# Rows ahead of transposes, values' eviction ahead of the exponential, and a first routing one round sooner, in a kernel for attention and a mixture of experts

## Chip, cores and metric

One core of a Trainium2 chip runs the whole program. The metric is device microseconds of one execution. The core has five engines that each work through their own instructions in order: TensorE (PE) for matmuls, VectorE (DVE), ScalarE (ACT), GpSimd (POOL) and SyncE (SP), which here issues most transfers. All data is float32 at the program's edges.

## What is computed

The reference takes q, k and v of shape (8, 8, 576, 64), does attention inside chunks of 64 positions, and sends the result through a mixture of experts with one expert for each token:

```python
scores = scale * np.matmul(q_c, k_c.transpose(0, 1, 2, 4, 3))      # chunks of 64
scores = scores - np.max(scores, axis=-1, keepdims=True)
attn = np.exp(scores)
attn = attn / (np.sum(attn, axis=-1, keepdims=True) + 1e-09)
out = np.matmul(attn, v_c)
x = out.transpose(0, 2, 1, 3).reshape(B * S, H * D)               # 4608 tokens x 512
logits = x @ w_gate + modality_bias[modality_id]                  # 8 experts
e_idx = np.argmax(logits, axis=1)
gate_w = softmax(logits)[np.arange(N), e_idx]
for e in range(E):
    mask = e_idx == e
    out[mask] = gate_w[mask, None] * (np.maximum(x[mask] @ w1[e], 0.0) @ w2[e])
```

The experts' two weight matrices are 512 x 1024 and 1024 x 512.

## The kernel before

**Stages.** Attention goes over 36 tiles of 128 tokens (two chunks of 64 for each of 8 heads), two tiles a round after the first two single ones. Behind it the tokens are worked expert by expert in slots of up to 384 tokens: a slot gathers its tokens' rows, turns them, and runs 8 steps f of a first matmul (`first`, tile `hp`) and a second one (`second`, tile `yb`). Weights and rows are split into a high and a low part so that three fast matmuls stand for one exact one.

**Order.** The program switches the planner off (`manual_schedule`): every engine gets its instructions in the order in which the Python code emits them. A wait of one instruction thus holds up all that was emitted behind it on the same engine. Buffers of one tag go round in turn; a new tile waits until the readers of the buffer's last tile are done. PSUM has two buffers of tag "s" (scores `sp`; later `hp`), two of tag "t" (transposed probabilities `ap`, values `xp`, some others), and the pair `yb`.

**A tile's way** (t is the tile):
- `scores(t)`: 16 matmuls of 64 x 64 into `sp`; DVE takes the maximum `mx` and subtracts it (`ex`).
- `exps(t)`: ACT takes the exponential in place; POOL adds the two halves into a ring tile `sr`.
- `sums(t)`: DVE sums `sr` (`sm`) and takes the reciprocal (`ris`).
- `transposes(t)`: 4 PE transposes of `ex` into `ap` (tag "t"); ACT copies them to `at`. The load of a later v tile is held back by a dependency on these transposes (`load_v(..., hold)`).
- `values(t)`: 16 matmuls of v and `at` into `xp` (tag "t"); ACT copies them to `xt` (the "eviction of values").
- `rows(t)`: 8 PE matmuls that turn `xt` back to token rows and give the router's partial logits, into `yb`; DVE scales them into `xr`.
- `put(t)`: ACT copies the partial logits (`lp`) and issues the write of `xr` to the DRAM table `xd`.

**A round** for tiles a and a+1 emits: transposes(a), rows(a-2), sums(a), put(a-2), rows(a-1), sums(a+1), put(a-1), v load of a+2, transposes(a+1), v load of a+3; scores of a+2 and a+3 with the q/k loads four tiles ahead; exps(a+2); values(a), values(a+1), exps(a+3). From round 8 to 22 each round also issues two writes that clear the token table (`clear_part`).

**Jobs.** Routing is written as generators. `advance()` takes one step of every generator in `jobs` and `pooljobs`; it is called after each `values`. `advance([pooljobs])` steps only the second list, twice more a round. `route(0)` covers tiles 0 to 13 and starts in round 14: step 1 scales the partial logits (POOL), step 2 adds them up (POOL, `lg`), step 3 takes the maximum (`gmx`) and the exponential (`ge`, ACT), steps 4 and 5 count tokens of each expert along the tiles (`scan`), step 6 does nothing, step 7 multiplies for the counts across partitions (`rp`, tag "t") and computes each token's place `pi`. It ends by adding `early_table` (which experts fill the first three slots, table `e_tab`, seven steps) and `scatter` (14 indirect writes `tab` by POOL, one a step). `route(1)`, for the other 22 tiles, runs in the expert stage.

**PLAN** says what is done ahead for the first slots at which tile, as t - 36 after values(t) and `advance()`: `locate` reads a slot's list of tokens from the table (SP: a register load and a DMA `tl`; it waits for the scatters), `gather` gets their rows (POOL: copy `tk`, then one indirect DMA a tile into `xg`), `fetch` loads weights (SP), `hi` and `lo` split them (ACT, DVE). `split(k)` transposes a quarter of the gathered rows of slot 0 on PE (`tp`, three transposes, one for each gather) and splits it on ACT and DVE.

Behind the last round stand split(0), rows(34), split(1), put(34), split(2), split(3), and then slot 0, which begins with `first` and takes rows(35) after it.

Of the kernel before, what the change touches and what calls it, by code (L numbers as in the profile page):

```python
# [8 lines left out]
F32 = mybir.dt.float32  # L9
# [10 lines left out]
P = 128  # L20
N = B * S
DM = H * D
E = 8
# [11 lines left out]
BUSY = 4  # L35
PLAN = {
    -9: {"fetch": [(0, 1), (1, 1)]},
    -7: {"locate": [(0,), (1,), (2,)]},
# [29 lines left out]
NEG = 1  # L68
# [21 lines left out]
def attention_moe(ctx: ExitStack, tc: tile.TileContext, qkv, mod, cst, bias, wcat, wfst, out):  # L90
# [168 lines left out]
    def sums(t):  # L259
        sm = wk.tile([P, H], F32, name="sm")  # L260
        V.reduce_sum(sm, sring[t % 4], axis=AX.X)  # L261
        V.reciprocal(ris[:, t], sm)

    def transposes(t):
        ex = st[t]["ex"].rearrange("p h k -> p (h k)")
        ap = ps.tile([P, NP, P], F32, tag="t", name="ap")
        for p in range(NP):
            hold = PE.transpose(ap[:, p, :], ex[:, p * P:p * P + P], ident)  # L268
        at = mp.tile([P, DM], F32, tag="yo", name="at", bufs=4).rearrange("p (a c) -> p a c", a=NP)
        A.copy(at, ap)  # L270
        st[t]["at"] = at
        return hold
# [15 lines left out]
    def rows(t):  # L288
        xt, ri = st[t]["xt"], ris[:, t]

        xr = wk.tile([P, NJB, NK, 32], F32, name="xr", bufs=4)
        fp = yb[t % 2].rearrange("p b (a c) -> p (b a) c", a=2)
        for p in range(NP):
            PE.matmul(fp[:, p, 0:GWC], xt[:, p, :], gw[:, p, :], start=True, stop=True)  # L294
        rb = ri.rearrange("p (a b) -> p a b", a=NP).unsqueeze(3)
        V.tensor_tensor(  # L296
            xr.rearrange("p (b j) a d -> p a b j d", b=2),
            fp[:, :, 0:P].rearrange("p a (b j d) -> p a b j d", b=2, j=2),
            rb.unsqueeze(4).to_broadcast([P, NP, 2, 2, 32]), ALU.mult)
        st[t] = fp, xr  # L300
# [11 lines left out]
    def route(g):  # L312
        t0, n = GROUPS[g]
# [44 lines left out]
        V.tensor_scalar_add(gs, gs, 1e-9)  # L358
        tg = tgs[g]
        V.reciprocal(tg.bitcast(F32)[:, :, 1], gs)  # L360
        for _ in range(2 if g < NEG else 5):
            yield
        rp = ps.tile([P, 2, 32, E], F32, tag="t", name="rp")
        PE.matmul(rp[:, 0, 0:n], ub, oh, start=True, stop=True)
        PE.matmul(rp[:, 1, 0:n + 1], ones, scan[i][:, off:off + n + 1], start=True, stop=True)
        V.tensor_tensor(base[g + 1], base[g], rp[:, 1, n], ALU.add)
# [380 lines left out]
    busy(BUSY)  # L747

    for a, n in [(0, 1), (1, 1)] + [(t, 2) for t in range(2, NT, 2)]:
        hold = transposes(a)  # L750
        if a > 1:
            for t in (a - 2, a - 1):
                rows(t)
                sums(t + 2)
                put(t)
            load_v(a + 2, hold)
            if 8 <= a < 24:
                clear_part()
            load_v(a + 3, transposes(a + 1))
            if 8 <= a < 24:  # L760
                clear_part()
            for g, (t0, m) in enumerate(GROUPS):
                if t0 + m == a:
                    jobs.append(route(g))
        else:
            if not a:
                exps(1)
            sums(a)
        advance([pooljobs])
        small = [t for t in (range(a + 2, a + 4) if a > 1 else (a + 2,)) if t < NT]  # L770
        for t in small:
            scores(t)
            load_qk(t + NB)
        if n == 2 and small:
            exps(a + 2)
        advance([pooljobs])
        for t in range(a, a + n):
            values(t)
            if small and (n == 1 or t > a):
                exps(small[-1])  # L780
            advance()
            plan(t - NT)
        if a == 2:
            prepare()
    split(0, "s")
    rows(NT - 2)
    split(1, "s")
    put(NT - 2)
    split(2)
    split(3)  # L790
# [81 lines left out]
```

## Time and profile before

| what | value |
|---|---|
| median of three runs | 563.65 us (563.55 to 563.82) |
| the profiled execution, its own time | 564.0 us |
| its span, first to last instruction | 562.1 us |
| mean granted clock of TensorE | 0.995 |
| busy PE / DVE / ACT / POOL | 549.6 / 360.9 / 244.4 / 175.2 us |
| DMA, mean over the span | 237 GB/s |

Times in a row of the profile are microseconds from the span's start. In a timeline a row reads: start, length, engine, line, operation, tile written and tiles read, shapes, count, and in brackets how long the engine had idled and what ended that. "PEld" is TensorE's weight load, which overlaps its matmuls; "SPq" and "ACTq" are transfers issued by SP and ACT. In a list of waits a row reads: who waited, for whom, microseconds in total, how often, the longest. In a table of stretches a row reads: from and to, length, busy time and instructions of PE, PEld, DVE, ACT and POOL, the clock granted to TensorE (1.00 is full speed), the DMA engines' busy share, GB/s. The attention stage is roughly the first 138 us, the experts the rest.

### The profile page before, as it was taken

How to read it: one execution, taken by the hardware profiler on the slowest of the kernel's cores; microseconds unless marked ns; L12 is line 12 of the kernel's file. 1: busy time of each engine (PE TensorE's matmuls, PEld its weight loads, DVE VectorE, ACT ScalarE, POOL GpSimd, SP SyncE). 2: the span in 40 equal slices, each digit the busy share in tenths (PEclk: the TensorE clock that was granted, in tenths of full speed). 3: DMA queues.
4: the chain of work that ended last, by engine and by line, in shares of the span. 5: the costliest groups of instructions: out<-in, count | busy, mean ns of one | idle time of the engine just before them, and what ended most of it. 6: DMA issues, size and time to landing. Idle time of an engine off the chain costs nothing.

```text
span 562.1 us, 12401 instructions
## 1 busy us (share of the span) xinstructions
PE 549.6 (98%) x4900; PEld 499.1 (89%) x4900; DVE 360.9 (64%) x633; ACT 244.4 (43%) x422; POOL 175.2 (31%) x182
## 2 busy tenths in 40 slices
PE   8999999998999999999999999999999999999995
PEld 6999989997889899899898999899899898998994
DVE  4777798966899665655656565565655656556751
ACT  3555554556434433443534434433434434435541
POOL 3322516742658754032220412213032220402011
PEclk9999999998999999999999999999999999999999
DMA  8999999998788649776683976748586683756500
GB/s 328 326 307 315 382 339 322 300 307 320 235 265 252 224 135 309 271 238 220 158 300 132 278 245 185 266 125 281 191 257 196 187 268 121 247 187 208 188 37 26
DMA packets 61409, 133.22 MB, mean 237 GB/s; under 512 B 11230, under 2 KB 31390, under 8 KB 54944
## 3 DMA queue, kind: packets, MB, share of 16 engines
q1 hardware_dynamic: 48368, 103.08, 56.3%
q0 software_dynamic: 7072, 19.18, 10.4%
q10 hardware_dynamic: 5904, 10.11, 4.9%
q8 instruction: 40, 0.66, 0.5%
q14 instruction: 25, 0.20, 0.1%
HBM read 102.16 MB, written 30.70 MB: 236 GB/s over the span
## 4 chain that ended last, share of the span: by engine, by line
PE 75%; issue 12%; DVE 4%; POOL 3%; DMA 2%; ACT 2%; ACTq 0%; POOLq 0%; DVEq 0%
PE yb L654 29%; PE hp L641 28%; PE yb L294 6%; PE sp L247 5%; PE xp L282 4%; PE ap L268 3%; POOL out L666 1%; DMA out<-yo,tk 1%; DMA qk<-in_qkv 1%; DVE xr L296 1%; PE yb L166 1%; DVE ex L251 1%; DVE mx L249 1%; DMA v<-in_qkv 1%; ACT ex L256 1%
## 5 line engine op out<-in xcount | busy, mean ns | idle before, releaser
L616 DVE TENSOR_TENSOR wl<-raw,wh 128x1024 fp32r<-128x1024 f32 (+1 forms) x106 | 129.6, 1224 | 37.2 <-ACT wh L612 37.2
L644 ACT ACTIVATE hh<-hp 128x384 fp32r<-128x384 f32 (+1 forms) x104 | 49.4, 475 | 217.7 <-PE hp L641 215.0
L641 PE MATMUL hp<-xl,wh 128*128 128x384 f32 (+1 forms) x416 | 136.7, 328 | 0.0
L641 PE MATMUL hp<-xh,wh 128*128 128x384 f32 (+1 forms) x416 | 136.4, 328 | 0.0
L641 PE MATMUL hp<-xh,wl 128*128 128x384 f32 (+1 forms) x416 | 136.3, 328 | 0.0
L645 DVE SCALAR_TENSOR_TENSOR hl<-hp,hh 128x384 fp32r<-128x384 f32 (+1 forms) x104 | 55.7, 536 | 111.0 <-ACT hh L644 111.0
L654 PE MATMUL yb<-wh,hl 128*128 128x512 f32 x296 | 117.4, 397 | 0.5 <-DVE hl L645 0.5
L654 PE MATMUL yb<-wh,hh 128*128 128x512 f32 x296 | 117.6, 397 | 0.0
L654 PE MATMUL yb<-wl,hh 128*128 128x512 f32 x296 | 116.8, 395 | 0.0
L666 POOL DMA_INDIRECT out<-yo,tk x37 | 46.9, 1267 | 222.5 <-DVE yo L665 214.8
L612 ACT CAST wh<-raw 128x1024 fp32r<-128x1024 f32 (+1 forms) x106 | 108.6, 1026 | 0.2 <-issue 0.2
L641 PEld LDWEIGHTS hp<-xl,wh 128*128 128x128 f32 x416 | 78.3, 188 | 4.2 <-DVE xl L586 0.3
L641 PEld LDWEIGHTS hp<-xh,wh 128*128 128x128 f32 x416 | 78.3, 188 | 3.8
L641 PEld LDWEIGHTS hp<-xh,wl 128*128 128x128 f32 x416 | 78.4, 189 | 0.0
L654 PEld LDWEIGHTS yb<-wh,hl 128*128 128x128 f32 x296 | 55.9, 189 | 14.9 <-DVE hl L645 1.5
L654 PEld LDWEIGHTS yb<-wl,hh 128*128 128x128 f32 x296 | 55.7, 188 | 9.5
L654 PEld LDWEIGHTS yb<-wh,hh 128*128 128x128 f32 x296 | 55.7, 188 | 9.1 <-ACT hh L644 0.2
L544 POOL DMA_INDIRECT xg<-xd,tk x37 | 41.2, 1113 | 24.5 <-issue 15.0
L257 POOL TENSOR_TENSOR sr<-ex 128x256 f32<-128x256 f32 x36 | 26.2, 728 | 70.3 <-ACT ex L256 70.2
L385 POOL DMA_INDIRECT tab<-tg,pi x36 | 39.6, 1099 | 15.0 <-issue 9.4
L294 PE MATMUL yb<-cs,xt 128*128 128x144 f32 x288 | 40.1, 294 | 0.0
L247 PEld LDWEIGHTS sp<-qk 64*64 64x64 f32 x1152 | 35.9, 137 | 3.9 <-DVE sm L261 1.8
(126 smaller groups left out, 524.7 us busy)
## 6 DMA issues: line engine op xcount, KB each, us to landing
raw<-in_wcat SPq DMA_DIRECT2D x48, 1024.0 KB, 6.6
qk<-in_qkv SPq DMA_DIRECT2D x36, 512.0 KB, 6.6
v<-in_qkv SPq DMA_DIRECT2D x36, 256.0 KB, 4.2
xd<-xr ACTq DMA_DIRECT2D x36, 256.0 KB, 2.9
xs<-xg SPq DMA_DIRECT2D x10, 768.0 KB, 5.0
xq<-xs SPq DMA_DIRECT2D x40, 192.0 KB, 4.1
raw<-in_wfst SPq DMA_DIRECT2D x4, 512.0 KB
raw<-in_wfst SPq DMA_DIRECT2D x2, 1024.0 KB
```

What stands on the lines that cost most here:

```text
L247: PE.matmul(sp[cs_, h, :], b[cs_, 0, hs], b[cs_, 1, hs], start=True, stop=True)
L257: G.tensor_tensor(sring[t % 4][:, :, 0:32], ex[:, :, 0:32], ex[:, :, 32:64], ALU.add)
L294: PE.matmul(fp[:, p, 0:GWC], xt[:, p, :], gw[:, p, :], start=True, stop=True)
L385: w = G.indirect_dma_start(tab, bass.IndirectOffsetOnAxis(ap=pi[:, j:j + 1], axis=0), tg[:, j, :], None, bounds_check=E * CAP - 1, oob_is_ ...
L544: G.indirect_dma_start(xg[:, t, :], None, xd[0:n, :], bass.IndirectOffsetOnAxis(ap=tk[:, t:t + 1], axis=0), bounds_check=n - 1, oob_is_err ...
L612: A.copy(hi, raw)
L616: (G if pool else V).tensor_tensor(lo, raw, hi.bitcast(F32), ALU.subtract)
L641: PE.matmul(hp, a[:, ks], b[:, k, 0:n], start=(m == 0), stop=(m == 3 * NK - 1))
L644: A.activation(hh[:, 0:n], hp, AF.Relu)
L645: V.scalar_tensor_tensor(hl[:, 0:n], hp, 0.0, hh.bitcast(F32)[:, 0:n], ALU.max, ALU.subtract)
L654: PE.matmul(ys[t], a[:, tsl], b[:, DM:2 * DM], start=(f == 0 and i == 0), stop=(f == NF - 1 and i == 2))
L666: w = G.indirect_dma_start(out, bass.IndirectOffsetOnAxis(ap=tk[:, t:t + 1], axis=0), yo, None, bounds_check=N - 1, oob_is_err=False)
```

## The change

Seven edits, with no instruction added or taken away:

1. In a round, `rows` of the earlier tile stands ahead of `transposes` of the new one (in before, transposes(a) came first and transposes(a+1) last).
2. `sums(a+1)` moves from between the rows to behind the scores.
3. `exps(a+2)` moves from ahead of values(a) to behind it, so that ACT gets the eviction `xt` of tile a first; exps(a+3) stays behind values(a+1).
4. `route(0)` has one empty step less, and round 18 takes one extra step of `jobs` ahead of its scores; `rp` so comes after values(18) where it came after values(20). Its PSUM tile takes tag "s" where it took "t".
5. The early table and the scatters follow: the first scatter comes after values(18), the last after values(25).
6. `locate` of the first three slots comes after values(28) where it came after values(29).
7. In the last round split(0) and split(1), both of tag "s", stand ahead of values(34).

```diff
 PLAN = {
     -9: {"fetch": [(0, 1), (1, 1)]},
-    -7: {"locate": [(0,), (1,), (2,)]},
+    -8: {"locate": [(0,), (1,), (2,)]},
     -6: {"gather": [(0, (0, 1))], "hi": [(0, 0)]},
...
-        for _ in range(2 if g < NEG else 5):
+        for _ in range(1 if g < NEG else 5):
             yield
-        rp = ps.tile([P, 2, 32, E], F32, tag="t", name="rp")
+        rp = ps.tile([P, 2, 32, E], F32, tag="s" if g < NEG else "t", name="rp")
...
     for a, n in [(0, 1), (1, 1)] + [(t, 2) for t in range(2, NT, 2)]:
-        hold = transposes(a)
         if a > 1:
-            for t in (a - 2, a - 1):
-                rows(t)
-                sums(t + 2)
-                put(t)
-            load_v(a + 2, hold)
-            if 8 <= a < 24:
-                clear_part()
-            load_v(a + 3, transposes(a + 1))
-            if 8 <= a < 24:
-                clear_part()
+            for t in (a, a + 1):
+                rows(t - 2)
+                load_v(t + 2, transposes(t))
+                if t == a:
+                    sums(t)
+                put(t - 2)
+                if 8 <= a < 24:
+                    clear_part()
             for g, (t0, m) in enumerate(GROUPS):
                 if t0 + m == a:
                     jobs.append(route(g))
+            if a == 18:
+
+                advance([jobs])
         else:
+            transposes(a)
             if not a:
                 exps(1)
             sums(a)
...
-        if n == 2 and small:
-            exps(a + 2)
+        if n == 2:
+            sums(a + 1)
+        if not small:
+            split(0, "s")
+            split(1, "s")
         advance([pooljobs])
         for t in range(a, a + n):
             values(t)
-            if small and (n == 1 or t > a):
-                exps(small[-1])
+            if small:
+                exps(small[t - a])
             advance()
             plan(t - NT)
         if a == 2:
             prepare()
-    split(0, "s")
     rows(NT - 2)
-    split(1, "s")
     put(NT - 2)
     split(2)
     split(3)
```

## The prediction

> **What bounds the kernel now.** I read the page first, then stretches of the span, then what TensorE (PE) waited for.
>
> ```profile
> span 562.1 us, 12401 instructions
> ...
> v<-in_qkv SPq DMA_DIRECT2D x36, 256.0 KB, 4.2
> ```
> ```profile
> 60.00:80.00 20.00, 19.34 (x431) 18.73 (x428) 17.10 (x41) 10.80 (x24) 8.62 (x11) 1.00 1.00 354
> ...
> 200.00:300.00 100.00, 100.00 (x502) 90.31 (x501) 58.21 (x78) 41.25 (x63) 26.82 (x25) 1.00 0.73 237
> ```
> The second window lies in the expert stage: PE is busy all of its 100 us, so whatever attention saves or loses arrives whole at the end, unless something there opens a gap. Now the dense attention round, from the chain of waits (start, length), and PE's waits over the span:
>
> ```profile
> 88.49 2.01 PE sp L247 x64
> 90.50 1.87 PE xp L282 x64
> 92.37 0.59 PE ap L268 x4
> 92.95 1.96 PE yb L294 x16
> 94.92 0.44 PE ap L268 x4
> ```
> ```profile
> PE ap L268 <- ACT xt L285: 3.1, 3, 2.2
> ...
> PE xp L282 <- ACT xt L285: 0.6, 1, 0.6
> PE yb L654 <- DVE hl L645: 0.5, 2, 0.3
> PE xp L282 <- ACT at L270: 0.3, 1, 0.3
> ```
> A round of two tiles is 6.87 us of PE work back to back, and the change doesn't alter that work. In attention there are only 3.1 + 0.6 + 0.3 = 4.0 us of waits to win. The longest has a sequel, seen in the timeline and in one stretch (the last three columns are granted clock, DMA share and GB/s):
>
> ```profile
> 121.22 0.18 POOL L540 COPY tk<-tl 128x3 int32<-128x3 int32 x1 [1.20 <-DMA tl<-tab]
> 122.54 1.07 POOL L544 DMA_INDIRECT xg<-xd,tk  x1 [1.13 <-DMA v<-in_qkv]
> ...
> 124.95 0.73 POOL L257 TENSOR_TENSOR sr<-ex 128x256 f32<-128x256 f32 x1
> 125.71 0.43 DVE L261 TENSOR_REDUCE sm<-sr 128x8 f32<-128x264 f32 x1 [2.44 <-POOL sr L257]
> 125.84 1.01 POOL L544 DMA_INDIRECT xg<-xd,tk  x1 [0.16 <-issue]
> 128.29 0.57 ACT L285 COPY xt<-xp 128x512 f32<-128x512 f32 x1
> 128.91 0.66 PE L268 MATMUL ap<-cs,ex 128*128 128x128 f32 x4 [2.22 <-ACT xt L285]
> ```
> ```profile
> 129.40:132.90 3.50, 3.50 (x17) 3.50 (x16) 2.18 (x5) 1.68 (x4) 0.85 (x2) 0.51 1.03 425
> ```
> Read it downwards: gathers on POOL hold up the small sum `sr` of an odd tile; VectorE (DVE), at `sums`, waits 2.44 us; the maxima and subtractions behind it are late, so is the exponential, so is `xt`, which stands behind it on ScalarE (ACT); PE stalls 2.22 us. Then PE runs 3.5 us at a granted clock of 0.51, which loses 3.5 x 0.49 = 1.7 us. The sum that can be won is 5.7 us.
>
> **The change part by part.** No instruction is added or removed; all is order, one PSUM buffer and one sooner step.
>
> *Eviction ahead of the exponential, `sums` of the odd tile behind the scores.* `xt` of a round's first tile now waits for PE alone, and the late `sr` no longer stands ahead of the maxima. This cuts the chain above: +2.2, and with it the slow clock, +1.7. The third `ap` wait, 3.1 - 2.2 - 0.7 = 0.2, is of the same sort: +0.2. The exponential goes back by one eviction (0.57) and is covered: in the new order (rows 0.98, transposes, rows, transposes) the transposes that want it come 0.98 us after the round's start, and it ends about 0.3 us after it. If that cover were gone, each round would lose what is over 0.7 us.
>
> *Rows ahead of transposes.* The same matmuls, alternating once more per round; 0 by the chain's rows, where 16 row matmuls between transposes take 1.96 and the 4 transposes behind them 0.44. Rows need `xt` as the transposes did (their PSUM buffer), so the wait moves, no more. A bound for the alternation is 0.59 - 0.44 = 0.15 a round, 2.5 us over 17 rounds; I take 0, as those rows show that very switch.
>
> *The v loads' hold.* The first of a round's two v loads now waits for transposes 1 us later; landing 4.2 us against use more than a round later hides it. The clears follow it as before.
>
> *First routing.* Its DVE work (gmx to scans, then the second scans to the reciprocal) is the same, but closer together. Before:
>
> ```profile
> 69.86 0.26 DVE L333 TENSOR_REDUCE gmx<-lg 128x14 f32<-128x112 f32 x1
> 69.89 0.66 PE L268 MATMUL ap<-cs,ex 128*128 128x128 f32 x4
> 70.46 0.30 ACT L336 ACTIVATE ge<-lg 128x112 f32<-128x112 f32 x1 [0.64 <-DVE lg L334]
> 70.66 0.57 ACT L285 COPY xt<-xp 128x512 f32<-128x512 f32 x1
> 72.56 0.68 DVE L296 TENSOR_TENSOR xr<-yb,ris 128x512 f32<-128x512 f32 x1
> 73.72 0.68 DVE L296 TENSOR_TENSOR xr<-yb,ris 128x512 f32<-128x512 f32 x1
> 74.32 0.42 DVE L261 TENSOR_REDUCE sm<-sr 128x8 f32<-128x264 f32 x1
> 74.89 0.64 DVE L249 TENSOR_REDUCE mx<-sp 128x8 f32<-128x512 f32 x1
> 75.57 0.69 DVE L251 TENSOR_TENSOR ex<-sp,mx 128x512 f32<-128x512 f32 x1
> 77.50 0.61 DVE L353 TENSOR_TENSOR scan<-scan 128x112 bf16<-128x112 bf16 x2
> 77.51 0.66 PE L268 MATMUL ap<-cs,ex 128*128 128x128 f32 x4 [0.66 <-ACT xt L285]
> 78.53 0.24 DVE L360 RECIPROCAL tg<-gs 128x14 f32<-128x14 f32 x1
> ```
> The waits of 0.66 and (PE's own, in the list) 0.6 both go: the first by the new ACT order, the second because `rp` no longer takes a "t" buffer between two values turns: +1.3. But a new one comes. After (times if all before stays): `sums` of tile 17 (0.57, from 74.32 to 74.89) now precedes gmx, which starts at 70.43. ACT's `ge`, 0.60 behind it, holds the second `xt` until 71.8 while PE wants its rows at 69.89 + 0.98 + 0.5 = 71.4: -0.4. On DVE, xr follows gmx by 2.70 as before, at 73.13; xr, sums, xr take 1.16 + 0.60: 74.89; then the extra step of round 18 (77.50 to 78.77: 1.27): 76.16; maximum and subtraction (0.68 + 0.69) end at 77.5. `rp` follows values(18) on PE, which ends at 71.8 + 0.98 + 0.45 + 2.0 + 0.95 = 76.2, and takes the older "s" buffer, that of scores(20), which this subtraction frees: PE waits 77.5 - 76.2 = 1.3. Behind it stand values(19), the next rows and everything. Together -1.7. That two buffers go round in turn is borne out by the second wait above: there `xp` had to wait for `xt` of the turn before, not for `rp`. Bounds: 0, if another buffer were given; -3.0, if it were the younger one, freed one pair later (1.3).
>
> *Lists one step sooner.* On SP nothing is issued between the two places, so the move alone passes no DMA: 0. What counts is that the scatters end a round (6.87) sooner, and the expert table too. SP's own waits, 100 to 145 us, and from its timeline the loads that came late by them:
>
> ```profile
> SPq L594 <- DVE e_tab L422: 2.8, 1, 2.8
> SPq L523 <- DMA tab<-tg,pi: 2.8, 1, 2.8
> ```
> ```profile
> 119.49 3.68 SPq L117 DMA_DIRECT2D v<-in_qkv  x4
> ```
> Both waits go; the first weights, the lists and the last four v loads (x4 in the row) are issued sooner, two of them by a round. None of PE's waits was for these.
>
> *Splits 0 and 1 ahead of the last values.* They fill the 0.3 us for which values waited on `at`: +0.3. But they need all three gathers landed, in order on PE. When? The new rounds 18 and 20 lose about as much as the old (1.7 against 1.3), and the rest run dense, so the round of tiles 34 and 35 starts at 128.9 - 2.2 = 126.7 (0.2 less for the third `ap` wait, 0.4 more for the other two); split 0 comes 2.99 later (0.59 + 1.96 + 0.44), at 129.7. The gathers stand behind `sr` of tile 32 on POOL, itself behind the exponential, now later: the round of tiles 30 and 31 starts at 126.7 - 2 x 6.87 = 113.0, its first values turn at 113.0 + 2.99 + 2.01 = 118.0, which is done some 1.1 later; that puts its eviction at 119.1, the exponential at 119.65 to 120.3, `sr` to 121.05. So `tk` runs at 121.1, as at 121.22 before, although its list is there earlier. The third gather follows the first by 3.30 and `tk` by 4.62 (before) or, without the 1.13 wait, 3.6: 124.7 to 125.7. Landing, by the software queue's packets (count, MB, share) in 130.4 to 132.4 and in 132.4 to 136.0, and by the landing times (least, median, most; one gather each) of two gathers for the next slots:
>
> ```profile
> q0 software_dynamic: 86, 0.26, 32.5%
> ...
> q0 software_dynamic: 1, 0.00, 0.0%
> ```
> ```profile
> DMA to landing us min/median/max: 4.7/4.7/4.7
> ...
> DMA to landing us min/median/max: 9.5/9.5/9.5
> ```
> The third gather thus landed by 132.4, up to 6.5 after issue, while weights shared the DMA engines; the kindest like case is 4.7. New landing: 129.4 to 132.2, a wait of 0 to 2.5. I take 1.0, nearer the kind end, because two v loads of 256 KB have left the time just ahead of it. -1.0.
>
> *Clock.* The wait of 0.66 left the clock at 1.00 (the window of 60 to 80 us), that of 2.22 didn't. New waits of 1.3 and 1.0 lie nearer the first: 0; -1.7 otherwise. [...]
>
> **Sum**: 2.2 + 1.7 + 0.2 + 1.3 + 0.3 = 5.7 won; 1.7 + 1.0 = 2.7 lost; the gain is 3.0. The profiled execution took 564.0 (span 562.1 and 1.9 around it), 0.35 over the median of 563.65; against that median the forecast is 560.6, against the profiled execution 561.0.
>
> **Rivals.**
> 1. *`rp` finds a free buffer* or DVE keeps up: its 1.3 is not paid, 559.3. For it: DVE has 17.10 of 20 us busy, not 20. Against: the sequence above has no gap.
> 2. *A new wait halves the clock*: the gather wait at 2.2 and 1.7 for the clock: 3.0 - 1.2 - 1.7 = 0.1, 563.5, no change. For it: 2.22 us did it before.
> 3. *Slower: split 0 waits on the gathers beyond cover.* Place: PE ahead of values(34). At the 9.5 us seen once, the third lands at 134.7: 5.0 instead of 1.0, and the clock 1.7: 3.0 - 4.0 - 1.7 = -2.7, 566.3. It turns the sign from a wait of 2.3 with the slow clock (3.0 + 1.0 - 1.7), a landing time of 6.8 from an issue at 125.2. Against: two of three such times are shorter.
> 4. *The gain doesn't get through*: DVE is loaded at the start of the expert stage and the 0.5 of PE's `hl` waits grows by what is won; 563.6. Against: that stage's order hangs on its own start.
>
> **Chances.** Forecast 0.54 (its own range, the split's wait from 0 to 2.5: 559.6 to 562.1), rival 1 0.14, rival 2 0.13, rival 3 0.09, rival 4 0.10. Below 0.2% (1.1 us) a measurement of this kernel can't tell a difference from none. Faster: 0.54 + 0.14 + 0.05 of rival 2 (a wait nearer 1) = 0.73; same: 0.08 of rival 2 and 0.08 of rival 4 = 0.16; slower: rival 3 and 0.02 of rival 4 = 0.11. The range leaves out rival 3 and the best of rival 1 (both costs at 0: 558.0): 558.5 to 563.8.
>
> **What would show it.** Right: no wait of `ap` or `yb` on `xt` at 120 to 130 us and clock 1.00 there; one PE wait at `rp` of about 1.3 us ending with a DVE subtraction, near 77.5; a PE wait at `tp` of about 1 us; the first `hp` matmul some 3 us sooner. Wrong: `rp` without a wait, `tp` waiting over 2.5 us, a stretch of clock 0.5, or an expert stage longer than before.

## The result: slower, 571.4 us, and the profile after

The kernel after takes 571.4 us (median, 567.51 to 572.05) where the kernel before takes 563.72 us beside it: a ratio of 1.0127, 95% interval 1.0105 to 1.0148. The forecast was 560.6, inside 558.5 to 563.8: wrong in sign. The profiled execution took 572.05 us (span 570.3), 8.05 us more than the one of before (564.0, span 562.1).

Where the time comes from is read in the order of the prediction: the waits of TensorE (PE) first. This is the list over 0 to 150 us of the kernel after (who, for whom, us in total, how often, the longest).

```profile
PE tp L584 <- DMA xg<-xd,tk: 3.0, 2, 1.9
PE yb L294 <- issue: 2.3, 1, 2.3
PE xp L282 <- issue: 1.9, 2, 1.0
...
PE rp L364 <- DVE ex L251: 0.9, 1, 0.9
PE yb L294 <- ACT xt L285: 0.4, 1, 0.4
PE yb L294 <- DMA cs<-in_cst: 0.3, 1, 0.3
PE xp L282 <- ACT at L270: 0.3, 1, 0.3
PE sp L247 <- issue: 0.3, 1, 0.3
```

The waits of before at `ap` and `xp` for `xt` (3.1 and 0.6) are gone, as predicted. In their place stand the wait at `rp` and one at `yb` (predicted, 1.3 together), 3.0 us of waits for the gathers, and 4.4 us of something new, "issue": PE stood still and nothing that the profile shows released it. PE's timeline of after gives the places:

```profile
28.03 1.55 PE L282 MATMUL xp<-at,v 64*64 64x64 f32 x46 [0.89 <-issue]
...
51.43 0.33 PE L282 MATMUL xp<-at,v 64*64 64x64 f32 x2 [0.96 <-issue]
...
74.51 1.25 PE L294 MATMUL yb<-cs,xt 128*128 128x144 f32 x8 [0.40 <-ACT xt L285]
...
80.00 0.22 PE L364 MATMUL rp<-oh,ub 128*128 128x112 bf16 x1 [0.87 <-DVE ex L251]
...
100.49 0.38 PE L247 MATMUL sp<-qk 64*64 64x64 f32 x5 [0.26 <-issue]
...
119.06 1.14 PE L294 MATMUL yb<-cs,xt 128*128 128x144 f32 x8 [2.31 <-issue]
...
137.91 0.33 PE L584 MATMUL tp<-cs,xg 128*128 128x128 f32 x1 [1.92 <-DMA xg<-xd,tk]
139.34 1.11 PE L584 MATMUL tp<-cs,xg 128*128 128x128 f32 x4 [1.10 <-DMA xg<-xd,tk]
```

**The stops with nothing to wait for.** Counted in the trace in PE's own order, waits for semaphores included, the four stops come at its instructions number 960, 1984, 4032 and 4800. Each is a multiple of 256 less 64. The page of after has a queue that fits this (packets, MB, share):

```profile
q8 instruction: 41, 0.67, 0.5%
```

41 packets of 0.67 MB are 16 KB each, and PE's 9957 instructions, counted in the same way, over 41 are 243 a packet. Now the DMA view of after in two stretches, one line of 110.9 to 116.7 us and one of 116.7 to 117.7 us:

```profile
DMA packets 678, 2.10 MB, mean 361 GB/s; under 512 B 77, under 2 KB 77, under 8 KB 677
...
q8 instruction: 1, 0.02, 6.0%
```

In the first stretch there is no packet of this queue, and 2.1 MB of other data move; in the second there is one, from 116.74 to 117.70 by the trace, and PE goes on at 119.06, 1.36 us behind its end. The same holds at the three others: the packet ends at 26.79, 49.98 and 99.10, and PE goes on 1.24, 1.45 and 1.39 us later. In the trace of before there is no such stop over 0.3 us in the first 150 us. The author reads this as PE out of instructions: each packet of this queue a block of some 256 of them, for which PE stood still 0.89 + 0.96 + 0.26 + 2.31 = 4.4 us. It is a reading of the places, the packets and their ends; no view shows what a packet holds. Such a stop is called a late block here.

**The splits.** POOL's and PE's timeline of after, around the last round:

```profile
126.92 0.65 POOL L540 COPY tk<-tl 128x3 int32<-128x3 int32 x1
...
128.16 1.08 POOL L544 DMA_INDIRECT xg<-xd,tk  x1 [0.60 <-POOL tk L540]
...
129.55 1.01 POOL L544 DMA_INDIRECT xg<-xd,tk  x1 [0.30 <-issue]
...
131.48 1.02 POOL L544 DMA_INDIRECT xg<-xd,tk  x1 [0.16 <-issue]
...
132.78 1.25 PE L294 MATMUL yb<-cs,xt 128*128 128x144 f32 x8
...
135.72 0.27 PE L584 MATMUL tp<-cs,xg 128*128 128x128 f32 x1
```

Split 0 comes 2.94 us into the round (2.99 predicted), and the third gather is issued 1.3 us ahead of it (1.0 to 2.0 predicted). But the second gather releases PE 8.4 us behind its issue and the third 7.9 us. Behind it PE is slow, as stretches of after show (from and to, length, busy time and instructions of five engines, granted clock, DMA share, GB/s):

```profile
116.00:120.00 4.00, 1.69 (x34) 1.74 (x31) 1.25 (x4) 1.99 (x4) 1.44 (x2) 1.00 1.05 407
...
120.00:130.00 10.00, 10.00 (x206) 9.60 (x206) 7.65 (x15) 5.85 (x14) 2.85 (x4) 1.00 0.67 201
...
138.30:145.10 6.80, 5.76 (x72) 5.32 (x73) 1.81 (x3) 2.65 (x5) 0.00 (x0) 0.50 0.46 175
```

The middle row is the stall that the change was to remove: PE is busy all the time at full clock where before it lost 2.2 us. The last row is 6.8 us at half clock; PE is busy for 5.76 of them, and half of that, 2.9 us, is lost.

**The rounds.** The starts of a dense round and of the next but one, after:

```profile
58.60 1.25 PE L294 MATMUL yb<-cs,xt 128*128 128x144 f32 x8
...
72.42 1.25 PE L294 MATMUL yb<-cs,xt 128*128 128x144 f32 x8
```

A round takes (72.42 - 58.60) / 2 = 6.91 us, 0.04 more than the 6.87 of before; 17 rounds make 0.7 us.

**The account.** Lost: 4.4 of late instructions, 3.0 for gathers, 2.9 - 1.7 = 1.2 of slow clock over that of before, 1.3 at `rp` and `yb`, 0.7 of alternation (rows and transposes taking turns more often). Won: 3.7 of waits for `xt`. Together 10.6 - 3.7 = 6.9 of the 8.05 us. This is the account of one execution. The first `hp` matmul of the experts stands at 138.38 before and 146.18 after, 7.8 later, and nothing of it is made up before the end (the spans differ by 8.2).

### The profile page after: what moved, and what is told of

The parts are those of the page before. It is cut to its first block, busy times and chain, and to the rows that moved or that the text cites. A ratio compares the mean times of both kernels' runs of the same rounds, so it can differ in the third digit from the quotient of the medians.

```text
span 570.3 us, 12433 instructions
## 1 busy us (share of the span) xinstructions
PE 552.5 (97%) x4899; PEld 500.9 (88%) x4900; DVE 364.5 (64%) x633; ACT 243.8 (43%) x422; POOL 174.5 (31%) x182
## 4 chain that ended last, share of the span: by engine, by line
PE 74%; issue 13%; DVE 4%; DMA 3%; POOL 3%; ACT 1%; POOLq 0%; ACTq 0%
PE yb L654 28%; PE hp L641 28%; PE yb L294 5%; PE sp L247 5%; PE xp L282 5%; PE ap L268 2%; DMA xg<-xd,tk 1%; DMA cs<-in_cst 1%; POOL out L666 1%; DMA raw<-in_wcat 1%; PE yb L166 1%; DVE wl L616 1%; ACT wh L612 1%; DVE ex L251 0%; POOL xg L544 0%
## 5 line engine op out<-in xcount | busy, mean ns | idle before, releaser
L654 PE MATMUL yb<-wl,hh 128*128 128x512 f32 x296 | 116.7, 394 | 0.0
L294 PE MATMUL yb<-cs,xt 128*128 128x144 f32 x288 | 43.6, 295 | 3.0 <-issue 2.3
L294 PEld LDWEIGHTS yb<-cs,xt 128*128 128x128 f32 x288 | 37.9, 192 | 4.5 <-issue 2.2
```

Source lines behind the costliest of these rows:

```text
L654: PE.matmul(ys[t], a[:, tsl], b[:, DM:2 * DM], start=(f == 0 and i == 0), stop=(f == NF - 1 and i == 2))
```

## The experiments

Each ratio is to the kernel before on the same chip in the same set of runs. The chips of the sets differ: the kernel before took 564.8 us on one, and 569.1 to 574.5 us on the others. On those others every kernel shows one thing more, here in the timeline of the kernel before with a late hold (below):

```profile
89.13 0.98 POOL L387 DMA_INDIRECT tab<-tg,pi  x1 [0.31 <-issue]
89.89 0.35 PE L247 MATMUL sp<-qk 64*64 64x64 f32 x4 [0.40 <-issue]
...
90.65 0.69 PE L247 MATMUL sp<-qk 64*64 64x64 f32 x16 [0.41 <-issue]
```

While POOL scatters to the token table, PE stops for 0.4 us again and again, some ten instructions apart (4 or 5 matmuls, besides weight loads), at places that are not 256 apart. Such trains of stops fall in the 64 x 64 matmuls of scores and values. Between 80 and 118 us they sum to 2.2 to 3.0 us in the kernels with the old order of rounds and to 3.8 to 5.0 us in those with the new one. What causes them was not found. So sizes of different sets aren't put side by side without saying so.

### Is the later hold of the v loads what delays the blocks?

The first idea was that a round's first v load, now held by later transposes, is issued at a worse time. Four kernels: two with the load held by an earlier matmul, one with a late hold in the kernel before, one with only the splits put back.

```diff
 # after, held early (also with the splits put back)
-load_v(t + 2, transposes(t))
+early = rows(t - 2)[1]; late = transposes(t)
+load_v(t + 2, early if t == a else late)
 # before, held late
-load_v(a + 2, hold)               # hold: transposes(a)
+load_v(a + 2, last matmul of rows(a - 2))
 # after, splits back
-    split(0, "s"); split(1, "s")  # ahead of values(34)
+    split(0, "s"); rows(NT - 2); split(1, "s")   # behind values(35)
```

> The changed kernel, with one dependency moved: the v load of a round's first tile is held by the second of the four row matmuls ahead of it, so that it is issued some 0.7 us into a round, as in the kernel before, where the change has it at 1.7 us (behind the transposes). In the changed kernel's trace PE stops four times for 'issue' (0.89, 0.96, 0.26, 2.31 us), each time at the same place modulo 256 of its instruction stream, just behind a 16 KB transfer on the instruction queue. Theory A (instruction blocks come late because the later v load pushes data into their way): the four stops shrink to under 1 us together, about 567 to 568 against 571.4. Theory B (the new order of PE's own work meets the blocks worse, whatever the loads do): the stops stay, 570 to 572.

> The kernel before, with the same dependency moved the other way: the v load of a round's first tile is held by the last row matmul of rows(a-2), some 1.7 us into the round as in the changed kernel. All else is as before. Theory A (late v loads starve the instruction queue): 'issue' stops of PE appear and the time goes up by 2 to 4 us, to 566 to 568. Theory B (it is the order of PE's work): within 0.5 us of 563.7.

> The changed kernel, with split(0) and split(1) back where they stood: split(0) behind the last values, split(1) behind rows(34). Theory S (the splits' new place costs the two waits on the gathers, 3.0 us, and the two stretches of half clock behind them, 3.4 us): 571.4 - 5 to 6, 565 to 566.5; clock 1.00 throughout attention. Rival (the gathers are so late that the wait only moves to the old place, and the half clock comes with it): 569 to 571.

> The changed kernel with both edits, the early hold of the v load and the splits back. Theories A and S together: 571.4 - 4 - 5.5, about 561 to 562.5, faster than both kernels. If B holds for the v load: as the kernel with the splits back alone. If the rival of S holds: as the kernel with the early hold alone.

Measured beside a kernel before of 574.52 us: held early 1.0121 (1.0019 to 1.0223); before held late 0.9939 (0.9898 to 0.9981); splits back 1.0052 (1.0000 to 1.0104); held early with splits back 1.0065 (1.0018 to 1.0112). An early hold won nothing and a late one cost nothing, so that this idea falls. Putting the splits back is the edit that seems to help: 1.0052 and 1.0065 with the splits back, against 1.0121 with them ahead and 1.0144 (1.0007 to 1.0281) for the whole change in the next set on that chip. The intervals overlap. Both edits together were expected faster than either kernel and fell short of that.

### One part alone

```diff
 # rounds only: before with edits 1 to 3       # routing only: before with edits 4 to 6
 # splits only: before with edit 7              # after, first weights two tiles later:
-    -9: {"fetch": [(0, 1), (1, 1)]},
+    -7: {"fetch": [(0, 1), (1, 1)]},
```

> The changed kernel once more, nothing edited, beside the four runs with edits, because those ran where the kernel before itself took 568.5 to 577.4 us. If the loss is a property of the change: slower than the kernel before of the same call by 1 to 1.5%. If it was the surroundings that day: within 0.5%.

> The kernel before with only the order inside the attention rounds changed (rows ahead of transposes, values' eviction ahead of the exponential, the odd tile's sums behind the scores, and with them the later hold of a v load); routing, lists and splits as before. The forecast's own ledger: the 2.2 us stall behind the late small sum and the 1.7 us of half clock go, so 563.7 - 4 and up to 0.8 back for the alternation seen in the changed trace (rounds of 6.91 against 6.87): 560 to 561 where before is 563.7. Theory I (the rounds' order makes instruction blocks late): 'issue' stops of PE of 2 to 4 us eat it: 563 to 565.

> The kernel before with only the routing one round sooner, its PSUM tile of tag s, the extra step in round 18 and the lists one step sooner; rounds and splits as before. Forecast's ledger: the two waits of rounds 18 and 20 (1.3 us) give place to one at the routing matmul of about 1.3, and the stall behind the gathers stays or shrinks with sooner lists: within 1 us of before. Theory W (weights of 1 MB asked for a round part sooner collide with instruction blocks): an 'issue' stop of 1 to 2.5 us near 115 to 125 us, 1 to 2.5 us slower.

> The changed kernel with the first two weight loads (1 MB) moved from behind values(27) to behind values(29), so that they follow the lists. Theory W: the longest of PE's 'issue' stops, 2.31 us at 119.06, where a block of instructions was asked for while those weights, two v loads and two q/k loads were under way, goes; about 2 us faster than the changed kernel of the same call. Rival: the block is late for the v and q/k loads alone; the stop stays, no difference.

> The kernel before with one part of the change alone: splits 0 and 1 ahead of the last two values turns. Theory L (the splits' cost is a wait for gathers, and hangs on how long these take to land behind other transfers, up to 8 us from issue): in the kernel before, the third gather is issued at 125.8 to 126.7, 2 to 3 us ahead of the last round, and split 0 would come some 3 us into it, near 132; with a landing of 6 to 8 us the wait is 0.5 to 3 us, time +0.5 to +3 us. The prediction's own sizes (landing 4.7 to 6.5): wait 0 to 1, gain 0.3, time -0.3 to +0.7 us.

| part | ratio | interval | before in the set |
|---|---|---|---|
| all (after again) | 1.0144 | 1.0007 to 1.0281 | 573.88 |
| rounds only | 1.0075 | 1.0024 to 1.0126 | 573.88 |
| routing only | 0.9977 | 0.9928 to 1.0027 | 573.88 |
| after, first weights later | 1.0122 | 0.9993 to 1.0250 | 573.88 |
| splits only | 1.0035 | 1.0011 to 1.0058 | 569.07 |

The rounds' order is slower by itself, where the forecast had most of its gain in it. Its trace has a late block of its own (1.62 us at 56.99), 4.9 us in trains, 3.41 us of half clock at 113.6, and a wait of 0.76 for a gather at the splits' old place. The routing is neither: its wait at `rp` came as predicted, and its gain doesn't show. In PE's timeline of routing only:

```profile
79.09 0.22 PE L364 MATMUL rp<-oh,ub 128*128 128x112 bf16 x1 [1.40 <-DVE ex L251]
```

The splits alone are slower too. In the timeline of splits only, the third gather and the transposes that need it:

```profile
132.38 1.01 POOL L544 DMA_INDIRECT xg<-xd,tk  x1 [0.16 <-issue]
...
138.34 0.38 PE L584 MATMUL tp<-cs,xg 128*128 128x128 f32 x2
140.41 0.66 PE L584 MATMUL tp<-cs,xg 128*128 128x128 f32 x4 [1.69 <-DMA xg<-xd,tk]
```

8.0 us from issue to use; the 0.5 to 3 us that were expected of a long landing fit (1.69 of wait, 2.0 us by the ratio), the prediction's own sizes (-0.3 to +0.7) don't. With the first weights later, the stop at instruction 4800 is gone and one of 1.33 us stands at 5056 instead: this late block moved with the first weights. The medians (579.18 against 582.57) lie in too wide a spread to call a gain.

Late blocks differ from one execution to the next. The whole change taken again has 1.62 us at 56.74 and 0.68 at instruction 4800, and none of the three near 28, 51 and 100 us. The old order has them too: 1.5 us in all in the trace of routing only, 0.7 in that of splits only.

### Lighter loads

If blocks and gathers come late behind data, half the data should cure it. These kernels leave out half of the later input: the scores of heads 4 to 7 take the columns of heads 0 to 3 again, and the values likewise. The tokens are so routed by other data, and the light kernels are compared with each other.

```diff
-SP.dma_start(b, qkv[t][:, 0:2])
+SP.dma_start(b[:, :, 0:DM // 2], qkv[t][:, 0:2, 0:DM // 2])   # from tile 4 on
-d = SP.dma_start(b, qkv[t][:, 2])
+d = SP.dma_start(b[:, 0:DM // 2], qkv[t][:, 2, 0:DM // 2])    # from tile 6 on
```

> The kernel after with lighter loads in attention: from tile 4 on a q/k load brings 256 columns of 512, and from tile 6 on a v load brings 256 of 512; the scores of heads 4 to 7 then take the columns of heads 0 to 3 again and the values likewise, so half of the input is left out and the routing goes by other data, while PE, DVE, ACT and POOL have the same instructions. Attention's transfers fall to about half, 350 GB/s to about 200. Theory I (PE's stops with nothing to wait for, which sum to 4.4 us after the change, are blocks of 256 instructions that arrive late behind queued data; and the splits wait for gathers that share the same DMA engines): the stops vanish, under 0.5 us in all, the wait of the splits falls under 1.5 us, and this kernel comes out no slower than the light kernel before, within 1 us or up to 3 us faster. Rival (the order itself costs PE time, whatever the transfers): the light kernel after is still slower than the light kernel before by 0.7 to 1.5% (4 to 8 us).

> The kernel before with the same lighter loads (half of the columns of each later q/k and v load left out, heads 4 to 7 and the second half of the values computed from the first half's data). It is the ground against which the light kernel after is read. By theory I the kernel before has almost no late instruction blocks where its trace was taken, so that it gains 0 to 2 us (the clock's stretch of 129 to 133 us stays, since POOL's order causes it); by the rival 0 to 2 us too. The difference of the two light kernels decides, not this one alone.

> The kernel before, unchanged, for a trace of it taken beside the others. Time: same as the kernel before, within 0.3%. Theory I: its blocks of PE instructions are in time or nearly so, stops with nothing to wait for under 1.5 us in all in the first 140 us, against 4 to 5 of the kernel after. Rival (such stops are ordinary and cost both kernels the same): 3 us or more here as well.

> The kernel before with its 8 warm-up matmuls of 512 columns at the start replaced by 32 of 128 columns: the same PE work ahead of the first scores, but 48 more PE instructions, so that all later borders between blocks of 256 instructions fall on other places of a round. Theory phase (whether a block comes late hangs on where its fetch falls among the transfers): other stops than in the kernel before, and a time that differs by 0.5 to 3 us either way. Rival (borders don't matter): within 0.3 us of the kernel before beyond the 0.2 us that the start itself may take, and no stops over 0.5 us.

This set's chip had no trains, and the kernel before took 564.76 us. Light after: 1.0110 (1.0061 to 1.0159), 570.66 us. Light before: 0.9944 (0.9927 to 0.9961), 561.77 us. So the change costs 8.9 us with half the data as well, and the theory's forecast of the time is refuted; its forecast of the late blocks holds only in part. PE's waits, light after:

```profile
PE tp L592 <- DMA xg<-xd,tk: 3.8, 2, 2.1
PE yb L302 <- ACT ex L263: 2.0, 1, 2.0
PE xp L290 <- ACT at L277: 1.5, 1, 1.5
...
PE rp L372 <- DVE ex L258: 0.9, 1, 0.9
...
PE yb L302 <- ACT xt L293: 0.4, 1, 0.4
```

and light before:

```profile
PE xp L290 <- ACT at L277: 1.9, 2, 1.4
PE ap L275 <- ACT xt L293: 1.4, 3, 0.7
...
PE xp L290 <- ACT xt L293: 0.6, 1, 0.6
```

The stops near 28, 51 and 100 us are gone, as they would be if the loads of q, k and v had made them; but they are gone with the full loads too, in the whole change taken again, so that this is not shown. That at instruction 4800 is still there (2.0 us; the list puts it down to an exponential, which those `rows` don't read, and the packet of the instruction queue ends 1.25 us ahead of it). It stands behind the first weights, which were not made lighter. The splits wait even longer. And three stretches of light after have a slow clock (the same columns as above):

```profile
110.00:120.00 10.00, 7.95 (x150) 7.82 (x149) 5.19 (x11) 3.52 (x8) 1.44 (x2) 0.84 0.79 226
...
130.00:140.00 10.00, 6.18 (x89) 5.39 (x84) 6.07 (x13) 4.67 (x10) 2.99 (x5) 0.86 0.93 367
140.00:150.00 10.00, 9.85 (x104) 9.16 (x103) 5.47 (x9) 4.68 (x9) 3.13 (x3) 0.80 0.48 154
```

10 x (0.16 + 0.14 + 0.20) = 5.0 us of clock. The splits' second wait, 1.76 us, lies in the last slow stretch, and PE loses nothing to the clock while it waits: 5.0 - 0.9 = 4.1. With the waits (2.0 + 3.8 + 1.5 + 0.9 + 0.4 = 8.6) and 0.7 of alternation that is 13.4, against 1.9 + 1.4 + 0.6 = 3.9 of waits in light before, which has no slow clock ahead of the experts' end: 9.5 more, and the spans (569.9 and 559.9) differ by 10.0. Most of the loss is thus accounted for by three things: one late block, the splits' waits, the clock behind both.

The kernel before again gives 1.0005 (0.9981 to 1.0028), and its trace answers a question that the prediction had got wrong: how long does a gather take where nobody waits for it? Its third gather, its first split, the weight load that waits for that gather, and the software queue's packets (count, MB, share) in 132 to 134 and 134 to 136 us:

```profile
126.65 1.01 POOL L545 DMA_INDIRECT xg<-xd,tk  x1 [0.16 <-issue]
...
135.40 0.76 PE L585 MATMUL tp<-cs,xg 128*128 128x128 f32 x3
135.83 0.14 PEld L585 LDWEIGHTS tp<-cs,xg 128*128 128x128 f32 x1 [0.23 <-DMA xg<-xd,tk]
```
```profile
q0 software_dynamic: 53, 0.16, 21.0%
...
q0 software_dynamic: 6, 0.02, 2.1%
```

The last packets run behind 134, 7.3 us and more after the issue, and the weight load for the third transpose is released at 135.8, 9.1 us after it. The old place of split 0, at 135.40, hid it all the same: no wait of a matmul shows.

With the blocks' borders shifted by 48 instructions (8 warm-up matmuls of 512 columns replaced by 32 of 128) the kernel before takes 1.0002 (0.9982 to 1.0021) of its time: in that order the place of the borders doesn't matter, and the theory of a mere phase gets no support.

### Moving the transfers of weights

```diff
 # weights behind the splits: after, with
-    -3: {"fetch": [(3, 1)], ...}, -2: {"hi": ...}
+    -3: {...}, -2: {"fetch": [(3, 1)], "hi": ...}
+        if g in (3, 4): after(d, [last transpose of split 1])
 # both moved: that, and the first weights at -7
 # route and hold: routing only, and the first v load held by rows(a - 2)
```

> The kernel after with two weight fetches (steps 3 and 4, 1.5 MB in all) held until split 1 is transposed, so that they can't share the DMA engines with the last gathers. Theory L: the gathers land 4 to 5.5 us after issue where they took about 8; the splits' wait falls from 3.0 to under 1 us, the clock's slow stretch behind it goes (3.4 us), and the kernel is 3 to 6 us faster than the kernel after, ratio to before 1.002 to 1.008. Rival (a gather takes that long whatever else runs): wait of the splits still 2.5 to 4 us, time as the kernel after, ratio 1.011 to 1.014. If the weights then come too late, a new wait in the first steps of slot 0 shows it.

> The kernel after with both transfers moved: the two fetches of the first weights two tiles later (from tile 27 to 29), and the fetches of steps 3 and 4 held until split 1. If late instruction blocks and late gathers, both behind weights, are the causes of most of the loss: ratio to before 0.997 to 1.004, PE's stops without a cause under 3 us in all, split wait under 1 us. If the order itself costs: 1.008 to 1.014.

> The kernel before with the first routing and lists sooner, as in the change, and with the hold of a round's first v load moved from its first transposes to the rows behind them; neither the rounds' order nor the splits move. The hold alone gave a ratio of 0.994 and the routing alone 0.998 where the kernel before took 574 us. If both add: 0.990 to 0.995 (559 to 562 us). If they win the same stall (POOL's late small sum near 127 us): 0.994 to 0.998.

Beside a kernel before of 569.07 us (with trains): weights behind the splits 1.0105 (1.0072 to 1.0139), both moved 1.0061 (1.0042 to 1.0079), route and hold 1.0000 (0.9985 to 1.0014). In the timeline of weights behind the splits:

```profile
135.29 1.02 POOL L544 DMA_INDIRECT xg<-xd,tk  x1 [0.16 <-issue]
...
141.40 0.33 PE L586 MATMUL tp<-cs,xg 128*128 128x128 f32 x1 [0.52 <-DMA xg<-xd,tk]
142.05 0.66 PE L586 MATMUL tp<-cs,xg 128*128 128x128 f32 x4 [0.33 <-DMA xg<-xd,tk]
```

With 1.5 MB of weights out of its way the third gather still takes 6.8 us, the second (issued at 133.36) 8.0. The weights are at most a small part of the landing; the theory that it is queueing behind them falls, and the rival, that a gather takes that long whatever else runs, is nearer. The splits' wait did shrink, to 0.8, since the third gather is here issued earlier against the round. The time hardly moved: among the chip's trains this kernel has a slow clock where the kernel with the splits alone, on the same chip, has none (80 to 100 us, first the one, then the other):

```profile
80.00:100.00 20.00, 17.64 (x309) 16.09 (x308) 13.46 (x41) 7.35 (x16) 11.41 (x13) 0.91 0.81 255
```
```profile
80.00:100.00 20.00, 18.10 (x376) 16.66 (x374) 15.53 (x46) 8.33 (x19) 9.61 (x11) 1.00 0.90 300
```

20 x 0.09 = 1.8 us. In the sets with trains all ten kernels that have the new order of rounds show 3.4 us or more of half clock between 80 and 118 us, and none of the four with the old order does (two of these have one in the expert stage). In PE's timelines a train holds up to four or five stops in a row with the new order and two or three with the old; why was not found.

With both transfers moved, late blocks fall to 0.2 us and the splits don't wait at all, and close to half of the loss is gone (1.0061 against 1.0105 beside it and 1.0127 for the change on a chip without trains). A new wait takes some of the gain, as ScalarE now waits for the later weights and `xt` stands behind that (its timeline, then PE's):

```profile
131.17 0.62 ACT L617 CAST wh<-raw 128x512 fp32r<-128x512 f32 x1 [1.90 <-DMA raw<-in_wfst]
```
```profile
132.33 1.25 PE L294 MATMUL yb<-cs,xt 128*128 128x144 f32 x8 [1.17 <-ACT xt L285]
```

The late hold, with an interval below 1 in its own set (0.9939), wins nothing together with the routing in this one, and was not run again alone: no version is shown twice to beat the kernel before.

### Parts under lighter loads

Edits 1 to 3 alone, and the whole change but the splits, with the lighter loads.

> The light kernel before (half of the columns of each later q/k and v load left out, heads 4 to 7 and half of the values from the first half's data) with one part of the change: the rounds' order. Read against the light kernels: before 0.994 of the kernel before, after 1.011. If the order costs only through late instruction blocks, these are gone with the lighter loads: within 1 us of the light kernel before, ratio 0.992 to 0.997. If the alternation of rows and transposes costs 0.05 us a round: +0.8 us, 0.9955. Rival (the order costs PE time by itself, as the 2.0 us of the rounds alone would have it): 0.998 to 1.000.

> The light kernel after with splits 0 and 1 at their old place (the same half of the loads left out). If the splits cost 4 us or more by their wait and the slow clock behind it, as 3.8 us of waits in the light kernel after say: 4 to 7 us faster than the light kernel after, ratio to before 0.999 to 1.004, with the late block of 2.1 us near 115 us still in it. Rival (the splits' wait only moves to another place): within 2 us of the light kernel after, 1.008 to 1.012.

Rounds only: 1.0073 (1.0029 to 1.0116). All but the splits: 1.0141 (1.0089 to 1.0193), beside 573.81 us. There is no late block in these two traces, so that the rounds' order costs time without them, which speaks for the rival there. But this chip had trains again (4.4 and 5.0 us of them between 80 and 118 us), with 6.8 and 3.4 us of half clock, and there is no light kernel before from the same set; the size of the order's own cost on a chip without trains stays open. The splits back were expected to bring 0.999 to 1.004 and did not: at their old place they waited for the third gather again, 1.54 us, and with the rounds only 1.18 us.

**Landing and cover.** Those waits follow from two times that every trace holds. One is the landing of the third gather, from its issue to the last of its sixteen semaphore updates: 6.7 to 9.6 us in all twenty traces, 7.2 in the trace of before and 7.8 in that of after, and no shorter with half the loads (8.0 to 9.6). The first of the three gathers lands after 3.6 to 8.2 us; they land one behind the other (at 129.36, 131.62 and 133.04 in before, 133.75, 137.87 and 139.29 in after). The second time is the cover, from the issue of the third gather to the first transpose of split 0: 8.8 to 10.3 us with the old rounds and the splits at their old place, 7.2 to 7.6 with the new rounds and the old place, and 4.2 to 7.0 with the new rounds and the splits ahead (4.2 in after). So both the new place and the new order of rounds take cover away, and PE waits where too little of it is left. The two kernels with the splits ahead that keep 6.8 and 7.0 us of it, both with the first weights later, don't wait.

## Why the prediction was wrong, point by point

- **The stall behind the late `sr`** (+2.2), **the third `ap` wait** (+0.2) and **the two waits of rounds 18 and 20** (+1.3): right. All are gone from PE's list.
- **The slow clock** (+1.7, and 0 for new waits): the stretch at 129.4 went, as predicted, but 6.83 us came at 138.28 and cost 2.9. The prediction put the new waits nearer to the 0.66 us that had left the clock alone; the fall came behind the first wait at `tp`, 1.92 us, with the second, 1.10, inside the slow stretch.
- **Wait at `rp` with `ge`** (-1.7): right in mechanism and place, 0.87 + 0.40 = 1.3; the "s" buffer was the one that the subtraction frees. 1.40 with the routing alone.
- **Values' `at` wait** (+0.3): right, it is gone from the last round. The 0.3 in the list of after stands at 10.26 us, in the first tiles.
- **Alternation at 0**: wrong by a little. 0.04 us a round, 0.7 in all; the bound of 0.15 held it.
- **Landing of the third gather** (4.7 to 6.5 after issue, wait 1.0): this is the step that failed, a term that was mis-sized. The landing took 7.8, the wait was 3.0 (two gathers), and the clock behind it cost the 2.9 above. This is the mechanism of rival 3, which put the turn of the sign at a landing of 6.8. The evidence quoted was misread: "landed by 132.4" took the time by which the queue's packets had thinned out, where the last semaphore update of that gather comes at 133.04, 7.2 us after its issue. The kind end of 4.7 came from gathers of the next slots, which weren't like it; no third gather of the twenty traces landed sooner than 6.7. With 7.2 the prediction's own sum gives a wait of 125.2 + 7.2 - 129.7 = 2.7, past its own turning point of 2.3.
- **What was not in the sum at all**: PE's four stops, 4.4 us in this execution, read above as blocks of its instructions that arrive late. Each transfer was asked whether its own reader waits for it; the instructions that PE itself reads were not thought of. Why the blocks come late stays open. The one at instruction 4800 stands in seven of the eight traces that have the new rounds and routing with the first weights at their place (0.65 to 2.44 us), and in the two with those weights asked for later it is gone and a stop stands at 5056; so it seems to hang on that transfer's place. The other three come and go between executions.
- **The v loads' hold and the lists one step sooner** (both 0): no run speaks against them. An early hold won nothing, a late one cost nothing, and the routing with its sooner lists is at 0.9977.
- **The sum**: 3.0 us were to be won and 8.05 were lost, 11.05 apart. The gathers' wait makes 2.0 of it (3.0 for 1.0), the clock 2.9, the late blocks 4.4, the alternation 0.7; `rp` and `ge` give back 0.4. That is 9.6; the rest is not accounted for.
- **The round of tiles 34 and 35 at 126.7**: it came at 132.78. The late blocks explain 4.4 of the 6.1 us, the alternation 0.7.
- **Rivals 1, 2 and 4**: `rp` did wait; half clock came 0.37 us behind the end of a gather wait of 1.92 us, where rival 2 had 2.2; the expert stage neither gave nor took.

The last experiments leave the order of rounds with a cost of its own that this account has only as 0.7 us of alternation. On a chip with trains the rounds alone cost 0.75%, of which the slow clock is about 1.5 us (half of the 2.9 us that PE is busy in it) and the longer trains 2 to 3 us.

## What to carry to other kernels

Before something is placed sooner, take the latest landing that any trace shows for what it reads, not the median, and see what the old place hid: here a landing of 7 to 10 us had 9 to 10 us of cover, the new order left 4, and that cost 3.0 us of waiting and 2.9 of slow clock. Read the landing from what waits for it or from the last semaphore update, not from the time by which a queue has thinned out. In a stretch where the DMA engines are busy nearly all the time (a share of 0.98 from 110.9 to 116.7 us of after), look for the instruction queue as one more reader: here four stops "issue", at places a multiple of 256 instructions apart, ended 1.24 to 1.45 us behind a packet of that queue. Data issued in front of it is the first suspect, but one trace without the stop proves nothing, as these stops come and go between executions. And a reordering that is meant to win a few waits must be tried part by part, since what it moves (blocks, gathers, scatters) can be worth more than what it wins.

## What the runs showed of the hardware

- **Instruction blocks.** In the trace of after PE stops for 0.26 to 2.31 us at its instructions 960, 1984, 4032 and 4800, and goes on 1.24 to 1.45 us after a 16 KB packet of the instruction queue ends. That the packet holds the instructions it stood still for is the author's reading. The profile may put such a stop down to another engine that had long been done (the row of 2.0 us in light after).
- **The clock.** Ahead of the kernels' end, half clock came in stretches of 3.41 us or twice that by the clock's records (3.41 from 129.48 us in before, 6.83 from 138.28 in after), and in the 3.41 us ahead of each PE had stood still for 1.2 to 2.9 us in all (2.2 in before, 2.0 in after). One stall doesn't decide: 2.22 us at 128.91 was followed by it in one trace of before, 2.16 us at the same place in the other was not; 2.31 us was not in after, 2.05 in light after was. What decides it was not shown.
- **Indirect gathers.** The third of three gathers of 128 rows each, issued within 3.6 us, landed 6.7 to 9.6 us behind its issue, with or without 1.5 MB of weights issued beside it and with full or half loads.
- **Trains of stops during scatters** on three of the four chips of the experiments, 2.2 to 5.0 us between 80 and 118 us, in every kernel run there, with a cause that stays open.
